# Local and global attention with a gated MLP on one Trainium2 core: batch 1 takes the chunk form of the later batches

## The chip, the cores and the metric

The kernel runs on one core of one Trainium2 chip. The core has five engines that run on their own and meet at semaphores: TensorE (PE: matmuls, with PEld for its weight loads), VectorE (DVE), ScalarE (ACT), GpSimd (POOL) and SyncE (SP). The metric is the device time of one execution in microseconds (us), as the median of the runs. The profile is of one execution of its own.

## The reference

Eight batches of eight heads; each head has 512 local and 32 global tokens of 64 dimensions. A global query attends to all 544 keys; a local query attends to the 32 global keys and to the local keys at a distance of at most 32. The result goes through a two-layer MLP (512 to 2048 to 512) with a quick-gelu between.

```python
k_all = concat([k_g, k_l]); v_all = concat([v_g, v_l])
out_g = softmax(scale * q_g @ k_all.T) @ v_all
mask = abs(pos[:, None] - pos[None, :]) <= 32
s_ll = where(mask, scale * q_l @ k_l.T, -1e9)
s_lg = scale * q_l @ k_g.T
out_l = softmax(concat([s_lg, s_ll])) @ concat([v_g, v_l])
x = concat([out_g, out_l]) as (B * S, H * D)
h = x @ w_in;  out = (h * sigmoid(1.702 * h)) @ w_out
```

## The kernel before, in words

**Tiling.** Four heads form a quad, so a batch has two (in the code `a` and `c`). Scores are computed with keys on the partitions and queries along the free dimension, in a first and a second round: `S(0)` and `S(1)` are the score matmuls, `X` the exponential on ACT, `M` the multiply with the 0/1 band mask, `U(0..2)` the matmuls that give the sum of the exponentials (unit 0, with a matrix of ones) and two halves of the output values, `Gm` the rows of the global queries, `R` the turned reciprocals of the sums, `XL` the normalised rows of x, `G` the global rows. `T`, `Tk` and `Tq` turn keys and queries by DVE transposes; `ext` puts the global queries (and keys) beside the local ones.

**Two forms of a quad.** Batches 0 and 1 use class `Quad`: four chunks of 128 local keys. The global keys are a part of their own: `gg` and `K` (both through `gk`, L367) compute their scores, `XK` (L417) the exponentials, `ekU` (L429) adds them to the sums, and `eg` (L398) spreads a small block for the global queries. Batches 2 to 7 use `Wide`: a chunk has 96 local and the 32 global keys, one chunk in five has 128 local keys, so the global keys need no step of their own. For it `Tk` copies a part of the turned keys (L525, called kcopy below), `Tq` copies a part of the queries (L535, qcopy), and `ext` writes the global keys between the local ones. The value tile (`load_v`, L97 and L99) holds the global value rows on partitions 96 to 127 of four of its five chunks, loaded four times from memory.

**The MLP.** `h_mm` and `h_step` (L624) are the first layer, 16 steps of four matmuls a batch; `h_act` is a tanh on ACT (L631) and a product on DVE (L632). `o_mm` (L649) is the second layer: four row blocks of 16 matmuls, here called output matmuls, and one copy on ACT (L663) for each block. `osteps` places quarters of a row block (four matmuls) between the parts of batch 1's attention.

**The order.** It is written out by hand: the schedule is manual, and each engine runs its instructions in the order of the program. Attention of batch b + 1 is woven into the output matmuls of batch b. All loads with a cast, so nearly all loads, go through POOL's queue (`load_rest`, then `load_v`, `load`, `load_g`): queries and keys of batch 1, the weights, the values of batch 1, queries and keys of batch 2, and so on. The program gives POOL's DMAs eight completion counters in turn, and each DMA waits on its counter's last user. Score banks: the pair of tiles `s0` and `s1` (four banks) from `spair()` is used by every score group in turn, and other stages borrow it; four more banks rotate under the name `p`.

**Batch 1 before.** ACT makes the two `near_mask` tables between the tanh's of batch 0 (L202). GpSimd makes the later batches' mask by six copies (L220) after the loads of batch 2's values. All four `M` of batch 1 are on DVE (L388). The transpose of batch 2's first queries stands in DVE's order between batch 1's second quad and its normalisation.

Of the kernel before, what the change touches and what calls it, by code (L numbers as in the profile page):

```python
# [20 lines left out]
def kernel(  # L21
# [68 lines left out]
    def load_v(b):  # L90
        if b < 4:
            nc.gpsimd.memset(v_view(b, 5)[:, :, :, :, D:], 1.0)
        vt = v_view(b, 5).rearrange("p u j c d -> p (u j) c d")
        vs, vg = (x[b].rearrange("h s d -> s h d") for x in (v_l, v_g))
        for c in range(5):
            n = 128 if c == 2 else 96
            nc.gpsimd.dma_start(out=vt[0:n, :, c, :D], in_=vs[FIRST[c] : FIRST[c] + n])  # L97
            if c != 2:
                nc.gpsimd.dma_start(out=vt[96:128, :, c, :D], in_=vg)  # L99

    rqg = consts.tile([128, NQ, D], BF16)
    rkg = consts.tile([128, NQ, D], BF16)

    rvg = consts.tile([128, 4, D + 2], BF16)

# [4 lines left out]

    def load_g(lo, hi, names="kqv"):
        for name, dst, src in (("k", rkg, kgf), ("q", rqg, qgf)):
            if name in names:
                nc.gpsimd.dma_start(out=dst[:, lo:hi, :], in_=src[:, lo:hi, :])
        if "v" in names:
            load_turned(nc.gpsimd, rvg[:, lo:hi, :D], vgf[:, lo:hi, :])

# [36 lines left out]
    for i in range(2):  # L154
        vtiles.append(consts.tile([128, 8 * 5 * (D + 2)], BF16, name="v%d" % i))
        nc.gpsimd.memset(v_view(i, 4)[:, :, :, :, D:], 1.0)
    nc.gpsimd.affine_select(
# [24 lines left out]
    WIN = ((0, 10), (6, 12), (14, 12), (22, 10))  # L182
    near_mask = consts.tile([128, 2, LW], BF16)
    mask = consts.tile([128, 2, MW], BF16)
# [14 lines left out]
    def make_near(c):
        nr = WIN[c][1]  # L200
        at = (0, 160, 0, 192)[c]
        nc.scalar.activation(near_mask[:, c // 2, at : at + 16 * nr].rearrange("p (t r) -> p t r", t=16),  # L202
                             near(bandt, c), AF.Copy)

# [41 lines left out]
    def load_rest():  # L246
        load_v2(0)
        n = d_ff // 4
        for part in range(4):
            for u in range(2):  # L250
                nc.gpsimd.dma_start(out=w_in_sb[:, part, 2 * u : 2 * u + 2],  # L251
                                    in_=w_in_r[u][:, :, part * n : part * n + n])
        for g4 in (1, 0, 2, 3):
            nc.gpsimd.dma_start(
                out=w_out_sb[:, 4 * g4 : 4 * g4 + 4, :].rearrange("p (g e) m -> p g (e m)", e=2),
                in_=w_out_r[:, 2 * g4 : 2 * g4 + 2, :])
            if g4 == 0:
# [9 lines left out]
        nc.gpsimd.dma_start(out=loaded[2][0], in_=kf[2])  # L267
        nc.gpsimd.dma_start(out=loaded[2][1][:, 1], in_=qf[2][:, 1])

# [13 lines left out]
    class Quad:  # L283
        def __init__(self, Q):
# [4 lines left out]
            self.x = xL[self.b]  # L289
            self.v = v_view(self.b, 4 if self.b < 2 else 5)[:, self.u]  # L290
            self.qt = qtiles[Q % 4]
# [78 lines left out]

        def X(self, rnd, between=None):
            e = self.E[rnd]
# [5 lines left out]
            for i in range(2):  # L378
                if i and between:
                    between()  # L380
                nc.scalar.activation(e[:, 2 * i : 2 * i + 2, :RW], self.ps[i][:, :, :RW], AF.Exp, scale=scale)  # L381
            if rnd == self.gr:
                nc.scalar.activation(e[:, 2, RW:], bank(self.ps, 2)[:, RW : RW + 32], AF.Exp, scale=scale)

        def M(self, rnd):
            at = 36 if rnd else 40
            e = self.E[rnd][:, :, at : at + LW]
            nc.vector.tensor_mul(e, e, near_mask[:, rnd : rnd + 1, :].to_broadcast([128, 4, LW]))  # L388

# [19 lines left out]

        def gg(self, rnd=0):  # L410
            self.gr = rnd
            self.gk(bank(self.ps if rnd else self.spt(0), 2)[:, RW : RW + 32], self.qg)


        def XK(self):
# [3 lines left out]
        def ekU(self, unit, ov=None):  # L419
# [4 lines left out]
            for j in range(4):  # L424
# [5 lines left out]
                                 start=first, stop=not first, skip_group_check=True)  # L430

        def ekUs(self, nxt=None, rnd=0, banks=(None, None, None)):
            if nxt:
                if rnd is not None:
                    nxt.gg(rnd)
                nxt.K(0)
            self.ekU(0, ov=banks[0])
            if nxt:
                nxt.K(1)
            self.ekU(1, ov=banks[1])  # L440
            self.ekU(2, ov=banks[2])

# [74 lines left out]
    class Wide(Quad):  # L517
        qc = None

        def Tk(self):  # L520
# [4 lines left out]
            nc.vector.tensor_copy(self.kT[:, 2:4, 0:96], self.kT[:, 0:2, 96:192])  # L525
            self.k = flat.bitcast(BF16).rearrange("p (m e) -> p m e", e=2)
# [304 lines left out]
    a.Tk()
    gTs[1] = moe.tile([128, FC, TB], BF16, name="gT")
    hps = [pbank("hp") for _ in range(2)]
    for fc, kcs in ((0, (0, 1)), (1, (0, 1)), (0, (2, 3)), (1, (2, 3))):
        h_mm(1, fc, hps[fc], kcs)
    pt = spair()
    hps += [bank(pt, j) for j in (2, 3, 0, 1)]
    for fc in range(2, 6):
        h_mm(1, fc, hps[fc], range(NKC))

    def on_act(out_, in_):
        nc.scalar.activation(out_, in_, AF.Copy)

    for fc in range(FC):
        if fc < 2:
            h_act(1, fc, hps[fc])
        elif fc in (2, 4):
            f = slice(fc, fc + 2)
            th = early[:, fc - 2 : fc]
            nc.scalar.activation(th, pt[1 - (fc - 2) // 2], AF.Tanh, scale=0.851)  # L850
            nc.vector.scalar_tensor_tensor(gTs[1][:, f, :], in0=th, scalar=1.0, in1=pt[1 - (fc - 2) // 2],
                                           op0=ALU.add, op1=ALU.mult)
        elif fc >= 6:
            h_step(1, fc)
        if fc == 1:
            transpose_g(4, 6, "q")
        if fc == 2:
            nq[1][1].G()
        if 3 <= fc <= 6:
            a.ext((fc - 3,), on_act)  # L860
        if 7 <= fc <= 9:
            c.ext((fc - 7,), on_act)
        if fc == 10:
            a.S(0)
            a.X(0, (0,))
        if fc == 11:
# [110 lines left out]
```

## Time and profile before

| what | value |
|---|---|
| time, median of 3 runs | 300.27 us (299.44 to 300.33) |
| the profiled execution's own time | 300.44 us |
| its span | 298.7 us |
| PE busy | 291.8 us, 98% of the span, 3407 matmuls |
| DVE busy | 217.1 us, 73% |
| ACT busy | 170.4 us, 57% |
| POOL busy | 80.4 us, 27% |
| DMA moved | 28.18 MB, mean 94 GB/s |

Times in the profile count from the start of the span. A line of a timeline holds start, duration, engine, source line, operation, output and inputs, the tile's shape, how many instructions are merged, and in brackets how long the engine stood idle before it and what ended that. Merged instructions overlap at their ends, so the step from one start to the next is the cost in sequence. The chain that ended last is followed back from the end of the program: each piece is what the next one waited for.

### The profile page before, as it was taken

Reading aid. Unit: us, or ns where it says so; the run is one execution under the profiler, and the core shown is the slowest. Engines: PE = TensorE matmul, PEld = TensorE weight load, DVE = VectorE, ACT = ScalarE, POOL = GpSimd, SP = SyncE. Lnnn points to the kernel's source line nnn. Section 1 sums busy time; section 2 is a strip of 40 time slices with the busy share of each in tenths; the row PEclk is TensorE's granted clock in tenths of the full one; section 3 lists DMA queues with packets and bytes.
Section 4 is the critical chain, followed back from the end, with each engine's and each line's share of the span. In section 5 each row is a group of like instructions: output and inputs, shape, how many; then the busy total and the mean of one; then the engine's idle time right before and its main releaser. Section 6 shows DMA issues by size and latency. Waiting matters only on the chain.

```text
span 298.7 us, 8149 instructions
## 1 busy us (share of the span) xinstructions
PE 291.8 (98%) x3407; PEld 150.1 (50%) x3407; DVE 217.1 (73%) x431; ACT 170.4 (57%) x280; POOL 80.4 (27%) x130
## 2 busy tenths in 40 slices
PE   7899999999999999999999999999999999999995
PEld 6444445445554455445454455445544455455653
DVE  7578857988978878797969878787879766683320
ACT  4838475397447736577357745676447651663421
POOL 8853655609754001800072003500000000000000
PEclk9999999999999999999999999999999999999999
DMA  7999999974999512980289114900230022101122
GB/s 204 162 196 210 188 168 217 151 137 28 149 204 155 106 37 63 131 144 20 54 81 187 36 38 82 116 0 16 59 72 0 2 54 56 35 1 28 45 69 72
DMA packets 59444, 28.18 MB, mean 94 GB/s; under 512 B 47504, under 2 KB 49808, under 8 KB 59408
## 3 DMA queue, kind: packets, MB, share of 16 engines
q0 software_dynamic: 51568, 17.57, 54.5%
q1 hardware_dynamic: 7360, 9.45, 12.1%
q10 hardware_dynamic: 480, 0.66, 0.7%
q8 instruction: 26, 0.43, 0.6%
q14 instruction: 10, 0.08, 0.1%
HBM read 36.31 MB, written 8.91 MB: 151 GB/s over the span
## 4 chain that ended last, share of the span: by engine, by line
PE 79%; DMA 12%; POOL 3%; DVE 3%; issue 1%; ACT 1%; ACTq 0%; DVEq 0%; POOLq 0%
PE op L649 33%; PE hp L624 33%; DMA rk<-in_k_l_dram 7%; PE ov L595 5%; PE s L569 4%; DMA rq<-in_q_l_dram 3%; DMA w_in_sb<-in_moe_w_in_dram 3%; PE s L624 1%; POOL v L244 1%; DVE xL L488 1%; PE op L661 1%; PE og L606 1%; DVE rs L483 0%; POOL w_in_sb L251 0%; ACT ob L663 0%
## 5 line engine op out<-in xcount | busy, mean ns | idle before, releaser
L649 PE MATMUL op<-w_out_sb,gT 128*128 128x512 bf16 x528 | 121.7, 380 | 0.0
L632 DVE SCALAR_TENSOR_TENSOR gT<-th,hp 128x512 bf16<-128x512 f32 (+1 forms) x136 | 87.0, 655 | 36.0 <-ACT th L631 35.5
L624 PE MATMUL hp<-xL,w_in_sb 128*128 128x512 bf16 x480 | 105.6, 379 | 0.2 <-DVE xL L488 0.2
L631 ACT ACTIVATE th<-hp 128x512 f32<-128x512 f32 (+1 forms) x136 | 77.5, 573 | 36.7 <-PE hp L624 34.0
L624 PEld LDWEIGHTS <-w_in_sb 128*128 128x128 bf16 x576 | 56.1, 98 | 64.7 <-issue 0.8
L649 PEld LDWEIGHTS <-gT 128*128 128x128 bf16 x528 | 49.3, 98 | 55.3 <-issue 0.9
L663 ACT ACTIVATE ob<-op 128x512 f32<-128x512 f32 (+2 forms) x35 | 20.4, 587 | 70.1 <-PE op L649 67.6
L97 POOL DMA_DIRECT2D v<-in_v_l_dram x30 | 24.0, 801 | 84.7 <-PE og L606 79.4
L580 ACT ACTIVATE e<-s 128x1016 bf16<-128x1016 f32 (+1 forms) x48 | 45.8, 1005 | 0.0
L585 DVE TENSOR_TENSOR e<-e,mask 128x1712 bf16<-128x1712 bf16 (+1 forms) x23 | 23.9, 1040 | 2.7 <-ACT e L580 2.1
L479 DVE STREAM_TRANSPOSE sT<-ov 128x512 f32<-128x512 f32 x15 | 10.7, 714 | 16.2 <-PE ov L595 14.4
L488 DVE TENSOR_TENSOR xL<-ov,rs 128x512 bf16<-128x512 f32 x29 | 18.7, 686 | 1.6 <-PE ov L455 0.4
L569 PEld LDWEIGHTS <-kT 32*128 32x128 bf16 x576 | 10.6, 93 | 10.4 <-issue 7.6
L381 ACT ACTIVATE e<-s 128x856 bf16<-128x856 f32 x12 | 10.1, 888 | 7.4 <-PE s L348 7.4
L99 POOL DMA_DIRECT2D v<-in_v_g_dram x24 | 13.9, 579 | 1.6 <-DMA rk<-in_k_l_dram 1.1
L569 PE MATMUL s<-q,kT 32*128 32x160 bf16 (+1 forms) x384 | 12.6, 246 | 0.0
L309 DVE STREAM_TRANSPOSE q<-rq 128x512 f32<-128x512 f32 (+1 forms) x17 | 11.4, 669 | 1.6 <-DMA rq<-in_q_l_dram 1.4
L523 DVE STREAM_TRANSPOSE kT<-rk 128x512 f32<-128x512 f32 x12 | 12.5, 1042 | 0.0
L483 DVE STREAM_TRANSPOSE rs<-rT 128x512 f32<-128x512 f32 x16 | 11.4, 711 | 0.6
L595 PE MATMUL ov<-e,v 128*32 128x128 bf16 (+3 forms) x576 | 11.0, 223 | 0.0
L624 PE MATMUL hp<-xG,w_in_sb 128*128 128x256 bf16 x64 | 9.6, 273 | 0.0
L595 PEld LDWEIGHTS <-v 128*32 128x32 bf16 x576 | 9.1, 97 | 0.0
(113 smaller groups left out, 202.8 us busy)
## 6 DMA issues: line engine op xcount, KB each, us to landing
out_dram<-ob SPq DMA_DIRECT2D x132, 64.0 KB, 2.5
rk<-in_k_l_dram POOLq DMA_DIRECT2D x6, 512.0 KB, 9.6
rq<-in_q_l_dram POOLq DMA_DIRECT2D x5, 512.0 KB, 7.4
v<-in_v_l_dram POOLq DMA_DIRECT2D x24, 96.0 KB, 4.5
w_in_sb<-in_moe_w_in_dram POOLq DMA_DIRECT2D x8, 256.0 KB, 8.2
w_out_sb<-in_moe_w_out_dram POOLq DMA_DIRECT2D x4, 512.0 KB, 10.3
v<-in_v_l_dram POOLq DMA_DIRECT2D x14, 128.0 KB, 6.4
rq<-in_q_l_dram POOLq DMA_DIRECT2D x5, 256.0 KB, 9.9
```

Of the source, the lines that this page charges most:

```text
L97: nc.gpsimd.dma_start(out=vt[0:n, :, c, :D], in_=vs[FIRST[c] : FIRST[c] + n])
L99: nc.gpsimd.dma_start(out=vt[96:128, :, c, :D], in_=vg)
L488: nc.vector.tensor_mul(self.x[:, 2 * self.u + h, :], self.st[1 + h], self.st["rs"])
L569: nc.tensor.matmul(bank(self.ps, j)[:, at : at + n], lhsT=self.k[p, KEYS[c] : KEYS[c] + 128, e], rhs=qs[p, :, :, e], start=(e == 0), stop= ...
L580: nc.scalar.activation(self.E[rnd][:, 2 * i : 2 * i + 2, :n], self.ps[i][:, :, :n], AF.Exp, scale=scale)
L585: eng.tensor_mul(e, e, mask[:, rnd : rnd + 1, :n].to_broadcast([128, 4, n]))
L595: nc.tensor.matmul(ov[32 * j : 32 * j + 32, :].rearrange("p (t r) -> p t r", t=16)[:, t0:t1, r0 : r0 + nr], lhsT=lv, rhs=self.E[rnd][:, j, ...
L624: nc.tensor.matmul(hp[:, : width(i)], lhsT=w_in_c[:, fc // 4, kc, fc % 4 // 2, :, fc % 2], rhs=(xL[i] if i < B else xG)[:, kc, :], start=( ...
L631: nc.scalar.activation(th[:, :n], hp[:, :n], AF.Tanh, scale=0.851)
L632: nc.vector.scalar_tensor_tensor(gTs[i][:, fc, :n], in0=th[:, :n], scalar=1.0, in1=hp[:, :n], op0=ALU.add, op1=ALU.mult)
L649: nc.tensor.matmul(op, lhsT=gTs[i][:, fc, tci * 128 : tci * 128 + 128], rhs=w_out_sb[:, fc, :], start=(first and fc == 4 * f4), stop=(fc = ...
L663: nc.scalar.activation(ob[:, lo:hi], op[:, lo:hi], AF.Copy, scale=0.5)
```

## The change

- Batch 1 becomes `Wide`: `nq = {1: (Wide(2), Wide(3)), ...}`. `gg`, `K`, `XK`, `eg`, `ekU` and `near_mask` are gone for it (`Quad` stays for batch 0).
- For its first quad, `ext`, kcopy and qcopy are done by ACT; for the second quad by DVE. The first rounds' masks of both quads are multiplied by GpSimd (`M(0, nc.gpsimd)`), the second rounds' by DVE.
- Its value tile has five chunks. The global value rows are loaded once (`load_vg1`) and copied by two ACT instructions into the other chunks (`copy_vg1`, between the exponentials of the first quad's two rounds). Its values come by five loads of 96 or 128 keys instead of four, one for each quad and half of the partitions.
- The six mask copies on GpSimd move to the load sequence, ahead of the last quarter of w_in.
- The loads of batch 2's keys and second queries move behind the first GpSimd multiply, those of batch 2's values and batch 3 behind the second.
- Batch 2's transposes and copies move behind the first products of batch 1's MLP, some of them from DVE to ACT; c's `Gm` now stands ahead of its `U`, the output quarters between the parts are placed anew, and the first eight h steps are held in four rotating and four score banks instead of two and four.

```diff
     def load_v(b):
-        if b < 4:
+        if b == 2:
...
-            if c != 2:
+            if c != 2 and b != 1:
                 nc.gpsimd.dma_start(out=vt[96:128, :, c, :D], in_=vg)
+    def load_vg1():
+        vt = v_view(1, 5).rearrange("p u j c d -> p (u j) c d")
+        nc.gpsimd.dma_start(out=vt[96:128, :, 0, :D], in_=v_g[1].rearrange("h s d -> s h d"))
+    def copy_vg1():
...
+        on_act(vt[96:128, :, 1:2, :D], src)
+        on_act(vt[96:128, :, 3:5, :D], src.to_broadcast([32, 8, 2, D]))
...
         for part in range(4):
+            if part == 3:
+                for m in MASKS:
+                    make_mask(m)
...
                 load(1, (0,))
                 load_g(2, 4)
+                load_vg1()
...
-        load_v2(1)
+        load_v(1)
         load(2, kq=False)
         nc.gpsimd.dma_start(out=loaded[2][1][:, 0], in_=qf[2][:, 0])
-        load_g(4, 8, "k")
-        load_g(4, 8, "q")
-        nc.gpsimd.dma_start(out=loaded[2][0], in_=kf[2])
-        nc.gpsimd.dma_start(out=loaded[2][1][:, 1], in_=qf[2][:, 1])
+        load_g(4, 8)
...
-        if fc in (5, 6, 8, 9):
-            make_near((5, 6, 8, 9).index(fc))
...
-    load_v(2)
-    for part in MASKS:
-        make_mask(part)
-    load(3)
...
-    nq = {1: (Quad(2), Quad(3)), 2: (Wide(4), Wide(5))}
+    nq = {1: (Wide(2), Wide(3)), 2: (Wide(4), Wide(5))}
     a, c = nq[1]
-    a.T()
     transpose_g(2, 4)
-    a.ext()
-    osteps(0, (0, 1), (0, 0), (1, 1), (1, 0), (2, 1))
+    a.Tk(False)
+    a.Tq(False)
+    a.ext((0, 1, 2), on_act)
+    a.kcopy(on_act)
+    a.ext((3,), on_act)
+    a.qcopy(on_act)
+    osteps(0, (0, 1), (0, 0), (1, 1), (1, 0), (2, 1), (2, 0))
     a.S(0)
-    a.gg()
-    a.K()
     a.X(0)
-    a.XK()
-    a.M(0)
-    a.eg()
-    c.T()
+    a.M(0, nc.gpsimd)
+    nc.gpsimd.dma_start(out=loaded[2][0], in_=kf[2])
+    nc.gpsimd.dma_start(out=loaded[2][1][:, 1], in_=qf[2][:, 1])
+    copy_vg1()
+    c.Tk()
+    c.Tq()
     c.ext()
-    osteps(0, (2, 0), (0, 2), (1, 2))
+    osteps(0, (0, 2), (1, 2), (2, 2))
     a.S(1)
     a.X(1)
     a.M(1)
-    osteps(0, (2, 2), (0, 3))
+    osteps(0, (0, 3), (1, 3))
     c.S(0)
     c.X(0)
-    c.M(0)
-    nq[2][0].Tq()
-    transpose_g(4, 6, "k")
-    osteps(0, (1, 3), (2, 3))
+    c.M(0, nc.gpsimd)
+    load_v(2)
+    load(3)
+    osteps(0, (2, 3), (3, 0))
     c.S(1)
-    a.ekUs(c, 1)
-    c.X(1, lambda: c.XK())
+    c.X(1)
     for unit in range(3):
         a.U(unit)
     a.R()
     c.M(1)
-    c.eg()
+    osteps(0, (3, 1), (3, 2), (3, 3))
     pt = spair()
-    a.Gm(bank(pt, 0)[:, 0 : D + 2])
-    osteps(0, (3, 0), (3, 1))
     a.XL(0)
     a.XL(1)
-    c.ekUs(banks=[bank(pt, unit + 1) for unit in range(3)])
-    for unit in range(3):
-        c.U(unit)
+    a.Gm(bank(pt, 1)[:, 0:128])
+    c.Gm(bank(pt, 1)[:, 128:256])
+    c.U(0, bank(pt, 0))
     c.R()
+    c.U(1, bank(pt, 2))
+    c.U(2, bank(pt, 3))
     c.XL(0)
     c.XL(1)
...
+    hps = [pbank("hp") for _ in range(4)]
+    for kcs in ((0, 1), (2,), (3,)):
+        for fc in range(4):
+            h_mm(1, fc, hps[fc], kcs)
     a.G()
-    c.Gm()
-    osteps(0, (3, 2), (3, 3))
+    c.G()
+    pt = spair()
+    for fc in range(4, 8):
+        h_mm(1, fc, bank(pt, (fc - 2) % 4), range(NKC))
...
         if fc == 1:
-            transpose_g(4, 6, "q")
+            transpose_g(4, 6)
+            a.Tk(False)
+        if fc in (2, 3):
+            a.ext((fc - 2,), on_act)
+        if fc == 3:
+            a.Tq(False)
+        if fc == 4:
+            a.kcopy(on_act)
+            a.ext((2,), on_act)
+        if fc == 6:
+            a.ext((3,), on_act)
+            a.qcopy(on_act)
...
         if i == 1:
-            c.Tk()
-        c.Tq()
-        if i > 1:
+            c.Tk(False)
+            c.Tq(False)
+        else:
+            c.Tq()
             c.ext((3,))
         a.S(1)
         a.X(1)
         if i == 1:
+            c.ext((0, 1, 2), on_act)
+            c.kcopy(on_act)
             c.ext((3,), on_act)
+            c.qcopy(on_act)
```

More of the change, by code (lines that the diff above doesn't have):

```diff
@@ L97, in load_v, with on_act @@
             nc.gpsimd.dma_start(out=vt[0:n, :, c, :D], in_=vs[FIRST[c] : FIRST[c] + n])
-            if c != 2:
+            if c != 2 and b != 1:
                 nc.gpsimd.dma_start(out=vt[96:128, :, c, :D], in_=vg)
+    def load_vg1():
+        vt = v_view(1, 5).rearrange("p u j c d -> p (u j) c d")
+        nc.gpsimd.dma_start(out=vt[96:128, :, 0, :D], in_=v_g[1].rearrange("h s d -> s h d"))
+    def copy_vg1():
+        vt = v_view(1, 5).rearrange("p u j c d -> p (u j) c d")
+        src = vt[96:128, :, 0:1, :D]
+        on_act(vt[96:128, :, 1:2, :D], src)
+        on_act(vt[96:128, :, 3:5, :D], src.to_broadcast([32, 8, 2, D]))
+    def on_act(out_, in_):
+        nc.scalar.activation(out_, in_, AF.Copy)
     rqg = consts.tile([128, NQ, D], BF16)
     rkg = consts.tile([128, NQ, D], BF16)
-    rvg = consts.tile([128, 4, D + 2], BF16)
+    rvg = consts.tile([128, 2, D + 2], BF16)
     def load_turned(eng, out_, in_):
@@ L109, in load_turned, with load_g @@
         eng.dma_start(out=out_[0:32], in_=in_[96:128])
-    def load_g(lo, hi, names="kqv"):
+    def load_g(lo, hi, names="kq"):
         for name, dst, src in (("k", rkg, kgf), ("q", rqg, qgf)):
@@ L114, in load_g @@
                 nc.gpsimd.dma_start(out=dst[:, lo:hi, :], in_=src[:, lo:hi, :])
-        if "v" in names:
-            load_turned(nc.gpsimd, rvg[:, lo:hi, :D], vgf[:, lo:hi, :])
     g32 = {}
@@ L155 @@
         vtiles.append(consts.tile([128, 8 * 5 * (D + 2)], BF16, name="v%d" % i))
-        nc.gpsimd.memset(v_view(i, 4)[:, :, :, :, D:], 1.0)
+        nc.gpsimd.memset(v_view(i, 4 + i)[:, :, :, :, D:], 1.0)
     nc.gpsimd.affine_select(
@@ L182 @@
     WIN = ((0, 10), (6, 12), (14, 12), (22, 10))
-    near_mask = consts.tile([128, 2, LW], BF16)
     mask = consts.tile([128, 2, MW], BF16)
@@ L197, in near @@
         return t[:, :, lo : lo + WIN[c][1]]
[L199 to L203, printed above, removed]
     MASKS = (
@@ L289, in __init__ @@
             self.x = xL[self.b]
-            self.v = v_view(self.b, 4 if self.b < 2 else 5)[:, self.u]
+            self.v = v_view(self.b, 5 if self.b else 4)[:, self.u]
             self.qt = qtiles[Q % 4]
@@ L369, in gk, with X @@
                                      start=(ee == 0), stop=(ee == 1), skip_group_check=True)
-        def X(self, rnd, between=None):
+        def X(self, rnd):
             e = self.E[rnd]
@@ L378, in X @@
             for i in range(2):
-                if i and between:
-                    between()
                 nc.scalar.activation(e[:, 2 * i : 2 * i + 2, :RW], self.ps[i][:, :, :RW], AF.Exp, scale=scale)
[L382 to L388, printed above, removed]
         def K(self, e=None):
@@ L408, in spt @@
             return self.pt
-        def gg(self, rnd=0):
-            self.gr = rnd
-            self.gk(bank(self.ps if rnd else self.spt(0), 2)[:, RW : RW + 32], self.qg)
         def XK(self):
@@ L430, in ekU @@
                                  start=first, stop=not first, skip_group_check=True)
[L432 to L441, printed above, removed]
         def U(self, unit):
@@ L518, with kcopy, qcopy, Tk @@
         qc = None
-        def Tk(self):
+        def kcopy(self, copy):
+            copy(self.kT[:, 2:4, 0:96], self.kT[:, 0:2, 96:192])
+        def qcopy(self, copy):
+            copy(self.qc[:, 4:20].bitcast(BF16), self.qt[:, 4:20, 10:22].bitcast(BF16))
+        def Tk(self, copy=nc.vector.tensor_copy):
             self.kT = att.tile([128, 4, 320], F32, name="kT", bufs=2)
@@ L524, in Tk @@
                                 loaded[self.b][0][:, self.u].bitcast(F32))
-            nc.vector.tensor_copy(self.kT[:, 2:4, 0:96], self.kT[:, 0:2, 96:192])
+            if copy:
+                self.kcopy(copy)
             self.k = flat.bitcast(BF16).rearrange("p (m e) -> p m e", e=2)
@@ L530, in near_q, with Tq @@
                 self.qc = att.tile([128, 20, 12], F32, name="qc", bufs=2)
-        def Tq(self):
+        def Tq(self, copy=nc.vector.tensor_copy):
             Quad.Tq(self)
             self.near_q()
-            nc.vector.tensor_copy(self.qc[:, 4:20].bitcast(BF16), self.qt[:, 4:20, 10:22].bitcast(BF16))
+            if copy:
+                self.qcopy(copy)
         def ext(self, parts=range(4), copy=None):
@@ L814 @@
     c.M(1)
-    c.eg()
+    osteps(0, (3, 1), (3, 2), (3, 3))
     pt = spair()
-    a.Gm(bank(pt, 0)[:, 0 : D + 2])
-    osteps(0, (3, 0), (3, 1))
     a.XL(0)
     a.XL(1)
-    c.ekUs(banks=[bank(pt, unit + 1) for unit in range(3)])
-    for unit in range(3):
-        c.U(unit)
+    a.Gm(bank(pt, 1)[:, 0:128])
+    c.Gm(bank(pt, 1)[:, 128:256])
+    c.U(0, bank(pt, 0))
     c.R()
+    c.U(1, bank(pt, 2))
+    c.U(2, bank(pt, 3))
     c.XL(0)
     c.XL(1)
+    gTs[1] = moe.tile([128, FC, TB], BF16, name="gT")
@@ L827 @@
+    hps = [pbank("hp") for _ in range(4)]
+    for kcs in ((0, 1), (2,), (3,)):
+        for fc in range(4):
+            h_mm(1, fc, hps[fc], kcs)
     a.G()
-    c.Gm()
-    osteps(0, (3, 2), (3, 3))
+    c.G()
+    pt = spair()
+    for fc in range(4, 8):
+        h_mm(1, fc, bank(pt, (fc - 2) % 4), range(NKC))
     a, c = nq[2]
[L831 to L842, printed above, removed]
     for fc in range(FC):
-        if fc < 2:
+        if fc < 4:
             h_act(1, fc, hps[fc])
-        elif fc in (2, 4):
+        elif fc in (4, 6):
             f = slice(fc, fc + 2)
-            th = early[:, fc - 2 : fc]
-            nc.scalar.activation(th, pt[1 - (fc - 2) // 2], AF.Tanh, scale=0.851)
-            nc.vector.scalar_tensor_tensor(gTs[1][:, f, :], in0=th, scalar=1.0, in1=pt[1 - (fc - 2) // 2],
+            th, ps = early[:, fc - 4 : fc - 2], pt[1 - (fc - 4) // 2]
+            nc.scalar.activation(th, ps, AF.Tanh, scale=0.851)
+            nc.vector.scalar_tensor_tensor(gTs[1][:, f, :], in0=th, scalar=1.0, in1=ps,
@@ L852 @@
                                            op0=ALU.add, op1=ALU.mult)
-        elif fc >= 6:
+        elif fc >= 8:
             h_step(1, fc)
         if fc == 1:
-            transpose_g(4, 6, "q")
[L857 to L862, printed above, removed]
+            transpose_g(4, 6)
[4 more added lines that the diff above has]
+            a.Tq(False)
@@ L870 @@
             load(4)
-            load_g(8, NQ, "kq")
+            load_g(8, NQ)
     def phase_o(i):
```

## The prediction

> **What bounds the kernel now.** I read first the page's busy times and the slices of the span, then the chain that ended last in order of time, then the timelines of PE, ACT, POOL and DVE between 32 and 72 us, where batch 1's attention runs.
>
> ```profile
> PE 291.8 (98%) x3407; PEld 150.1 (50%) x3407; DVE 217.1 (73%) x431; ACT 170.4 (57%) x280; POOL 80.4 (27%) x130
> ...
> DMA  7999999974999512980289114900230022101122
> ```
>
> PE is busy nearly all the time, so a gain must be PE work that goes or one of its few waits. The DMA engines are full until about 60 us (the first eight slices of 7.5 us). The chain shows where a landing, not PE, decided:
>
> ```profile
> 37.62 9.89 DMA rq<-in_q_l_dram
> ...
> 47.53 0.72 DVE q L309
> ...
> 54.25 1.30 DVE xL L488 x2
> ...
> 55.59 0.81 PE hp L624 x3
> ...
> 64.17 0.58 PE s L569 x23
> ...
> 69.17 0.56 PE s L569 x23
> ```
>
> Batch 2's query load lands at 47.5; its transpose stands in DVE's queue ahead of batch 1's normalisation, so batch 1's last xL comes late and the h matmuls of batch 1, begun at 54.03 (52.25 + 8 x 0.222), lose 0.64: their first eight last from 54.03 to 56.40 instead of 8 x 0.216 = 1.73. I measure the change at the last line: batch 2's second score group now starts at 69.17, and behind it everything is one steady run of PE work, the same in both kernels.
>
> **PE work.** The timeline gives the old form of batch 1 (the separate global-key work is L367 and L429):
>
> ```profile
> 36.92 0.66 PE L348 MATMUL s<-q,kT 32*128 32x200 bf16 x16
> 37.51 0.22 PE L367 MATMUL s<-qgT,kgT 32*32 32x32 bf16 x8
> 37.58 0.62 PE L367 MATMUL kb<-q,kgT 32*32 32x512 bf16 x8
> ...
> 50.85 0.68 PE L455 MATMUL s<-e,ones 128*32 128x160 bf16 x16
> ```
>
> From start to next start: four score groups 0.59 + 0.60 + 0.59 + 0.59, global scores 0.62 (36.92's group ends at 37.51, next work at 38.13), the mixed global stretch 46.27 to 47.07 = 0.80, ekU 50.10 to 50.85 = 0.75, U 0.93 and 1.12, Gm 0.27 and 0.28: 7.14. The new form is read from batch 2 in the chain: 0.56 + 0.58 + 1.20 + 0.16 = 2.50 a quad, 5.00 for both. So 2.14 of PE work goes; the 64 output matmuls stay (64 x 0.2224 = 14.23). If nothing waited, h would begin at 32.44 + 14.23 + 5.00 = 51.67 and the mark come 13.82 + 0.57 later, at 66.1: 3.1 sooner, of which 0.64 is the lost wait and 0.3 small gaps. The question is what of it other engines leave.
>
> **ACT.** The four near_mask copies go (about 0.4 each between tanh's, off PE's path: worth nothing, PE was full there). Batch 1's exponentials grow, and copies come:
>
> ```profile
> 41.52 1.66 ACT L381 ACTIVATE e<-s 128x856 bf16<-128x856 f32 x2 [1.67 <-PE s L348]
> ...
> 69.77 1.89 ACT L580 ACTIVATE e<-s 128x992 bf16<-128x992 f32 x2
> ```
>
> The wide first round takes 1.93 (73.90). At the start qgT is out at 34.7, kT at 35.9, q at 36.6 (DVE's transposes from 34.53); the three small copies, kcopy (192 elements, between the rows of 0.30 and 0.60; I take 0.35), 0.42 and qcopy 0.5 end by 37.2, before a.S(0) at 37.78 (24 instead of 20 output matmuls first). So they cost nothing; without those four extra matmuls, 0.3. a.X(0) runs 38.4 to 40.35. The two global-value copies have no row on 32 partitions; by their 512 and 1024 elements they take 0.6 and 1.0 (rows of 128 partitions; a quarter of that if partitions counted). I take the full price: a.X(1) then runs 41.8 to 43.7, and c.S(0), due at 43.36, has its last two banks at 43.7. Then two output copies (0.5 each) and c.X(0), 44.55 to 46.5; c.S(1), due at 46.06, ends at 47.1; c.X(1) ends at 49.15. ACT thus costs PE 0.9 here. The copies moved to ACT in batches 1 and 2's second quads (about 1.8 after a.X(1)) end just as c.S(0) of batch 2 wants them, 0 to 0.3; I take 0.
>
> **POOL and the loads.** POOL is one queue, and each of its DMAs waits for the landing of the one eight issues back:
>
> ```profile
> 39.36 0.75 POOL L114 DMA_DIRECT2D rqg<-in_q_g_dram  x1 [0.38 <-DMA rk<-in_k_l_dram]
> 42.37 0.70 POOL L267 DMA_DIRECT2D rk<-in_k_l_dram  x1 [2.25 <-DMA w_out_sb<-in_moe_w_out_dram]
> ...
> 67.40 3.32 POOL L585 TENSOR_TENSOR e<-e,mask 128x1760 bf16<-128x1760 bf16 x1 [8.41 <-issue]
> ```
>
> The last w_out load, issued at 33.67, lands 8.4 later, at 42.07; now the eighth issue behind it is rk, in the new kernel (five value loads instead of four) it is rqg. So rqg is issued at 42.1 to 42.8, and behind it stands the first GpSimd mask: 42.8 to 46.1 (3.32), though its exponentials are there at 40.35. Then the two loads of batch 2 (0.70 + 0.57), then the second mask, 47.45 to 50.75. Its first reader, c.Gm, is due at 51.24: the multiplies on GpSimd are just hidden by themselves. The six mask copies (2.33, from 55.30) now stand ahead of the third w_in pair. POOL spent over 5 us waiting for landings between 14.6 and 24.7, and at 16.4 five w_in loads are still in flight, the last landing at 22.7: I take 0, and 2.3 if that cover is gone. The value loads and vg are as many bytes as before and land by 46.6, and the first value matmuls start at 47.6. rk of batch 2 is issued 3.7 later but queues behind loads until 48.4; its transpose comes at 58. The nine value loads of batch 2 and load(3) now follow the second multiply, 50.8 to about 58.5, for readers from 71 on: 0.
>
> **DVE.** Batch 1's second quad is transposed when its rk lands (39.1) and, with six copies, ready by 42.2, ahead of c.S(0): 0; a load later by more than 1.2 would show there.
>
> **Where GpSimd and DVE meet.** Four DVE copies that met a POOL DMA issue (ending at 36.86) lasted 0.36 to 0.61 each and ended together at 36.87 to 36.89; alone the same four took 0.43 in all:
>
> ```profile
> 35.21 1.65 POOL L244 DMA_DIRECT2D v<-in_v_l_dram  x2
> ...
> 36.26 0.63 DVE L319 COPY q<-qgT 128x40 f32<-128x40 f32 x4
> ...
> 41.73 0.43 DVE L319 COPY q<-qgT 128x40 f32<-128x40 f32 x4
> ```
>
> A POOL multiply beside a DVE multiply has no row: each DVE mask may cost its 1.05, or wait for the POOL multiply's end. I take the wait, since the nearest row shows one. [...] Then a.M(1), ready at 43.7, runs 46.1 to 47.15, and a.U starts at 47.2, which costs 0.1. c.M(1), ready at 49.4 behind a.R, runs 50.75 to 51.8, and c.Gm waits from 51.24 to 51.85. DVE then does a.XL (1.3), c.R (1.75), c.XL (0.65 each): third kc at 55.5, where PE wants it at 54.95; last xL at 56.1.
>
> **The end of the stage.** Behind it DVE owes, without a pause, two G (1.3), four products (2.4), transposes (0.35 + 1.05 + 0.65) and two double products (1.1 each): 7.95, until 64.05, since the score banks of batch 2 are the ones that the second double product reads. PE could start that score group at 63.4. Then 0.57 and 20 matmuls (4.32): the mark at 69.0 against 69.17. The sum: -3.1 (PE and old waits) + 0.9 (ACT) + 0.1 + 0.6 (c.Gm) + 0.6 (xL) + 0.7 (banks) = -0.2. The profiled execution took 300.44 (span 298.7), 0.17 above the median of 300.27; so **300.44 - 0.2 - 0.17 = 300.1**.
>
> **Rivals.**
> - *The multiplies run side by side.* c.M(1) then ends at 50.45, c.Gm and xL do not wait, last xL at 54.9, banks at 62.85, mark at 67.8: -1.4, **298.9**. For it: the products (L632) at 67.8 to 69.8 kept their 0.68 beside POOL's multiply, but one of their inputs is in PSUM. Against: the copies above.
> - *All is hidden,* with short ACT copies and banks in time: -3.1, **297.2**. Against it: DVE's 7.95 hardly shrinks.
> - *POOL's queue comes late:* slower. If the 2.33 of mask copies is not absorbed, w_out lands at 44.4, both POOL multiplies and all behind them move by 2.3: **302.4**; half of it gives 301.2. It decides from 1.1 of lateness on. For it: c.Gm already waits on that chain, so each us counts in full. Against: POOL's waits at 17 to 32 us, and full DMA engines.
> - *No net effect by other small waits,* near 300.3.
>
> **Chances.** About 0.3% (0.9 us) is what a measurement of this kernel can tell from no change. Forecast 0.47 (of it 0.08 faster, 0.33 same, 0.06 slower), side by side 0.25 (0.21 faster, 0.04 same), all hidden 0.05 (faster), late queue 0.15 (0.13 slower, 0.02 same), small waits 0.08 (0.02, 0.04, 0.02). Faster 0.36, same 0.43, slower 0.21. The range goes from between the second and third case, 298.4, to 301.6 on the side of the late queue.
>
> **What would show it.** In the new profile: two POOL multiplies at about 43 and 47.5, the first behind rqg, waiting for w_out; the DVE mask beside each lasting 2 us or more, or starting late (right), or 1.05 beside it (first rival); exponentials of ACT back to back from 38 to 49; PE waiting at c.S(0), c.S(1), c.Gm and at batch 2's first score group; U with 72 matmuls in 1.20. Wrong would be: w_out landing after 43, value loads after 47.6, or h of batch 1 beginning later than 54.

## The result and the profile after

The changed kernel takes 301.38 us (median of 22 runs, 300.15 to 304.46); the kernel before, run beside it, 299.67 (22 runs, 299.28 to 302.28). The ratio is 1.0063, interval 1.004 to 1.0086: **slower by 0.6%**, where 300.1 was forecast against 300.27. The profiled execution took 303.67 (span 302.0) and is one of five, of 22, in which the mean granted clock was 0.989 to 0.994 instead of 0.998 to 1.0; those five took 303.2 to 304.5, the other 17 took 300.15 to 301.9. So the profile shows the loss in its strongest form, and a second profile of the same kernel (below) is read beside it. Of one later kernel (the loads of batch 2 ahead of the first multiply) four runs of twelve were over 1.5% above its fastest, 305.8 to 306.5, and its ratio is that of the other eight.

The page of after, busy times and slices:

```profile
PE 288.5 (96%) x3390; PEld 150.2 (50%) x3431; DVE 215.0 (71%) x421; ACT 173.1 (57%) x284; POOL 87.1 (29%) x131
...
PEclk9999999799999999999999999999999999999999
DMA  7999999950999711990269512900220012101113
```

PE is busy for 3.3 us less than before (291.8), and yet the span is 3.3 longer: PE stands idle. The timeline of PE in after shows where (in brackets: idle time before, and what ended it):

```profile
43.77 0.53 PE L557 MATMUL s<-q,kT 32*128 32x160 bf16 x14 [0.25 <-ACT e L568]
...
46.57 0.28 PE L557 MATMUL s<-qc,kT 32*128 32x108 bf16 x6 [0.18 <-ACT e L568]
...
51.36 0.55 PE L583 MATMUL s<-e,ones 128*32 128x128 bf16 x24
51.73 0.75 PE L583 MATMUL s<-e,v 128*32 128x128 bf16 x38
54.71 0.35 PE L583 MATMUL s<-e,v 128*32 128x72 bf16 x10 [2.23 <-issue]
54.99 5.32 PE L612 MATMUL hp<-xL,w_in_sb 128*128 128x512 bf16 x15
...
66.85 0.53 PE L557 MATMUL s<-q,kT 32*128 32x160 bf16 x16 [0.50 <-DVE gT L830]
```

In the middle of the 72 value matmuls of the second quad PE stops for 2.23 us, after 62 of them, and goes on with the last ten. The first 14 matmuls of `U(2)` had run, and `U(1)` had read all the exponentials that the last ten read again. "issue" says that the profile shows nothing that PE waited for. Batch 1's h begins at 54.99 instead of the 53.3 forecast. The chain that ended last has the same pause in its midst:

```profile
51.54 0.94 PE s L583 x62
52.48 2.23 issue
54.71 0.35 PE s L583 x10
55.06 0.76 PE hp L612 x3
```

There is a second pause later, behind batch 2's first values (timeline of PE):

```profile
78.64 0.39 PE L637 MATMUL op<-w_out_sb,gT 128*128 128x512 bf16 x1 [0.67 <-DVE rT L461]
```

PE's last matmul ended at 77.97 and this one began at 78.64: 0.67. The profile puts the wait down to a reciprocal on DVE, but that had ended at 78.15, 0.49 before. In a kernel below (the split kernel) the same matmul starts at 74.21, right behind the values, while that reciprocal lasts until 74.45; so it does not wait for it.

**The measure of the prediction**, the start of batch 2's second score group, is 69.10 in the timeline of PE of before and 71.84 in after. (The chain puts it 0.07 later in both; below, "the mark" is the timeline's.) The row of before, then that of after:

```profile
69.10 0.28 PE L569 MATMUL s<-qc,kT 32*128 32x108 bf16 x8
...
71.84 0.28 PE L557 MATMUL s<-qc,kT 32*128 32x108 bf16 x8
```

**Where the loads and multiplies came.** POOL's timeline of after:

```profile
40.55 0.74 POOL L127 DMA_DIRECT2D rqg<-in_q_g_dram  x1 [1.71 <-DMA w_out_sb<-in_moe_w_out_dram]
41.31 3.33 POOL L573 TENSOR_TENSOR e<-e,mask 128x1760 bf16<-128x1760 bf16 x1
...
46.61 3.32 POOL L573 TENSOR_TENSOR e<-e,mask 128x1760 bf16<-128x1760 bf16 x1 [0.72 <-ACT e L568]
```

rqg did wait for w_out, but that landed at 40.27, 1.8 sooner than assumed, so both multiplies ended before anything needed them. DVE's two masks beside them (DVE's timeline of after):

```profile
43.82 1.74 DVE L573 TENSOR_TENSOR e<-e,mask 128x1712 bf16<-128x1712 bf16 x1 [3.30 <-ACT e L568]
...
49.40 1.43 DVE L573 TENSOR_TENSOR e<-e,mask 128x1712 bf16<-128x1712 bf16 x1
```

Alone this multiply takes 1.04 (a row of it stands below). Here each ended about 0.9 behind the end of GpSimd's: 45.56 against 44.64, and 50.83 against 49.93. They were held, as forecast.

**PE had run out of instructions.** The trace lists a DMA queue of kind "instruction", and the page of after counts it:

```profile
q8 instruction: 27, 0.44, 0.6%
```

Twenty-seven packets of 16 KB. By the page's 3390 matmuls and 3431 weight loads, a packet holds about 253 of these, some 127 pairs of a weight load and a matmul (an estimate from these three counts, which takes all 27 packets for PE's). Counted along PE's program, the two pauses stand at its 734th and 988th weight load, 254 = 2 x 127 apart. From the starts and durations of the single packets, and with the blocks laid so that one ends at each pause (in before, which has none, by the same count of loads, so its two entries are good to some tenths of a us):

| kernel, profile | PE enters the block of loads 607 to 733 | next packet runs | PE has used up the block | PE goes on |
|---|---|---|---|---|
| before | 48.00 | 51.36 to 52.34 | 57.53 | at once |
| after | 48.01 | 52.31 to 53.27 | 52.48 | 54.71 |
| after, second profile | 48.61 | 52.44 to 53.37 | 53.08 | 54.69 |

In before, too, the packet comes 3.4 us after the block is entered, but there the block holds many long matmuls (0.216 each) and lasts 9.5 us. In after it holds 116 small matmuls (8 to 17 ns each: `Gm` 0.33 for 40, `U` 1.20 for 72) beside 11 long ones, and is used up in 4.5 us. PE goes on 1.4 us after the packet's end, at both pauses (53.27 to 54.71; 77.24 to 78.64). My theory from here: **the denser form eats its instructions faster than they come.** The rivals: the wait hides some data (loads, the ACT copies, a mask), or it is the late clock that costs.

### The profile page after: what moved, and what is told of

Same layout as the page of the kernel before. It is cut to its first block, busy times and chain, and to the rows that moved or that the text cites. A ratio compares the mean times of both kernels' runs of the same rounds, so it can differ in the third digit from the quotient of the medians.

```text
span 302.0 us, 8148 instructions
## 1 busy us (share of the span) xinstructions
PE 288.5 (96%) x3390; PEld 150.2 (50%) x3431; DVE 215.0 (71%) x421; ACT 173.1 (57%) x284; POOL 87.1 (29%) x131
## 4 chain that ended last, share of the span: by engine, by line
PE 85%; ACT 4%; DVE 3%; issue 2%; ACTq 0%
PE hp L612 36%; PE op L637 35%; PE ov L583 5%; PE s L557 5%; ACT e L568 2%; PE s L612 1%; DVE gT L620 1%; ACT ob L651 1%; DVE gT L830 1%; PE op L649 1%; PE og L594 1%; ACT v L112 1%; PE s L583 0%; DVE e L573 0%; DVE kT L509 0%
## 5 line engine op out<-in xcount | busy, mean ns | idle before, releaser
L637 PE MATMUL op<-w_out_sb,gT 128*128 128x512 bf16 x498 | 119.1, 379 | 2.4 <-DVE rT L461 0.7
L568 ACT ACTIVATE e<-s 128x1016 bf16<-128x1016 f32 (+1 forms) x56 | 53.5, 1006 | 2.0 <-PE s L557 1.9
L97 POOL DMA_DIRECT2D v<-in_v_l_dram x35 | 28.3, 815 | 82.3 <-PE og L594 81.5
L573 DVE TENSOR_TENSOR e<-e,mask 128x1712 bf16<-128x1712 bf16 (+1 forms) x25 | 27.1, 1082 | 6.0 <-ACT e L568 5.4
L557 PEld LDWEIGHTS <-kT 32*128 32x128 bf16 x672 | 12.8, 93 | 13.2 <-issue 9.7
L557 PE MATMUL s<-q,kT 32*128 32x160 bf16 (+1 forms) x448 | 15.0, 246 | 0.8 <-DVE gT L830 0.5
L509 DVE STREAM_TRANSPOSE kT<-rk 128x512 f32<-128x512 f32 x14 | 14.6, 1039 | 1.6 <-DMA rk<-in_k_l_dram 1.6
L573 POOL TENSOR_TENSOR e<-e,mask 128x1760 bf16<-128x1760 bf16 x3 | 10.0, 3322 | 12.9 <-issue 12.2
L583 PEld LDWEIGHTS <-v 128*32 128x32 bf16 x672 | 10.5, 97 | 2.4 <-issue 2.4
```

The lines of the kernel that those rows point to most:

```text
L557: nc.tensor.matmul(bank(self.ps, j)[:, at : at + n], lhsT=self.k[p, KEYS[c] : KEYS[c] + 128, e], rhs=qs[p, :, :, e], start=(e == 0), stop= ...
L568: nc.scalar.activation(self.E[rnd][:, 2 * i : 2 * i + 2, :n], self.ps[i][:, :, :n], AF.Exp, scale=scale)
L573: eng.tensor_mul(e, e, mask[:, rnd : rnd + 1, :n].to_broadcast([128, 4, n]))
L583: nc.tensor.matmul(ov[32 * j : 32 * j + 32, :].rearrange("p (t r) -> p t r", t=16)[:, t0:t1, r0 : r0 + nr], lhsT=lv, rhs=self.E[rnd][:, j, ...
L637: nc.tensor.matmul(op, lhsT=gTs[i][:, fc, tci * 128 : tci * 128 + 128], rhs=w_out_sb[:, fc, :], start=(first and fc == 4 * f4), stop=(fc = ...
```

## The experiments

A ratio compares a kernel with the runs of before that were timed beside it. The medians of these are 300.03 (23 runs), 299.67 (35) and 299.66 (30).

**The changed kernel again.** No edit.

> The changed kernel once more. Theory A (PE runs out of instructions in the dense stretch of small matmuls at 48 to 52.5 us, because the next 16 KB block of its program comes over the loaded DMA engines; the pause then halves PE's granted clock for some us): the pause sits at the same matmul pair (the 734th) with 1 to 3 us, whether or not the clock drops; time 300 to 304, about 0.6% above before. Theory B (a data wait that the profile does not name: a landing or a bank): the pause has the same place too; this run alone does not tell them apart, it gives the spread.

301.67, ratio 1.0053 (1.0033 to 1.0073). Its profile (span 300.4, clock 0.999), timeline of PE:

```profile
52.32 0.76 PE L583 MATMUL s<-e,v 128*32 128x128 bf16 x38
54.69 0.35 PE L583 MATMUL s<-e,v 128*32 128x72 bf16 x10 [1.61 <-issue]
54.97 3.63 PE L612 MATMUL hp<-xL,w_in_sb 128*128 128x512 bf16 x15
```

The pause is at the same matmul, 1.61 long, and again at the 988th load, 0.85. The clock stayed full: the 15 h matmuls took 3.63 here and 5.32 in the first profile. That 1.7 is the whole difference of the two marks (70.13 and 71.84). So the halved clock comes on top, and the pauses come without it.

**Other places of the block ends.** A hundred matmuls of batch 0's MLP, all ahead of the pauses, are each made two of half the columns. That adds 100 pairs ahead of batch 1, and so moves every block's end within its matmuls; the work is the same.

```diff
...
+            n = width(i)
+            w_ = n // 2 if i == 0 and fc >= 4 else n
+            for lo in range(0, n, w_):
...
+                                 rhs=(xL[i] if i < B else xG)[:, kc, lo : lo + w_],
...
+            w_ = 256 if i == 0 and (tci < 3 or st == 12) else 512
+            for lo in range(0, 512, w_):
...
```

> 100 matmuls of batch 0's MLP, all before 46 us, are split in two of half the columns: the same arithmetic and about the same PE time, but every later instruction stands 100 pairs further back in the program, so that the block of about 127 pairs that now begins at 48.0 and runs dry at 52.5 begins with the pair that ran at 45.0 and ends with the one at 51.1. Theory A: the fetch has 6 us instead of 4.5, the pause of 2.2 shrinks below 0.6, PE's clock stays at 1.0, h of batch 1 begins near 52.7 instead of 55.0; time about 298.5 to 299.5. Theory B: no data moved, the pause stays at 52.5 with 2.2 us; time 301.4.

This first form sets the start flag for both halves of a bank, and its output is off by a relative 0.115: part of those sums is left out. 299.24, ratio 0.9978 (0.9966 to 0.999); no pause, mark at 68.31. The form with one start flag for a bank:

> The split of the run before with the accumulation flags set so that each half adds up rightly; the instructions, their number and their order are the same. Theory A: as in that run, no pause behind the second quad's U and none at the next block's end (76 us), clock 1.0, time 299.0 to 299.6, about 0.8% below the changed kernel. If that run's gain came from its arithmetic, this one is at 301.4.

299.34, ratio 0.9994 (0.9981 to 1.0008). Timeline of PE:

```profile
51.54 0.55 PE L583 MATMUL s<-e,ones 128*32 128x128 bf16 x24
51.90 0.91 PE L583 MATMUL s<-e,v 128*32 128x128 bf16 x48
52.74 3.44 PE L615 MATMUL hp<-xL,w_in_sb 128*128 128x512 bf16 x13
```

Both pauses are gone, the mark is at 68.15, and the time is 2.0 us below the changed kernel's, which had lost 1.7. Below, this is "the split kernel". Nothing that the value matmuls read was touched, which speaks against a hidden wait for data. The packet behind the new block's entry at 44.52 came at 44.96, the next (51.22) at 51.59.

**The same split in the kernel before.**

> The same split in the kernel before, as a control for the split itself: 100 more matmul pairs before 46 us, the same arithmetic. Theory A: in the kernel before no block runs dry, so the split brings nothing unless it puts a boundary into a dense stretch: within 0.4 of before. If splitting matmuls is a gain of its own (weights loaded twice, finer waits), about 0.8 faster than before.

299.96, ratio 1.0004 (0.9994 to 1.0014): the split by itself brings nothing. Its mark is at 68.33, though, 0.77 sooner than in the profile of before: PE had no 0.64 at 55.

**Long matmuls between the small ones.** Of the changed kernel, the first two parts of four h steps are put between `c.U(0)` and `c.U(1)`, and `Gm` behind `U`.

```diff
+    c.U(0, bank(pt, 0))
+    c.R()
...
+    for fc in range(4):
+        h_mm(1, fc, hps[fc], (0, 1))
+    c.U(1, bank(pt, 2))
+    c.U(2, bank(pt, 3))
     a.Gm(bank(pt, 1)[:, 0:128])
     c.Gm(bank(pt, 1)[:, 128:256])
-    c.U(0, bank(pt, 0))
-    c.R()
-    c.U(1, bank(pt, 2))
-    c.U(2, bank(pt, 3))
...
-    for kcs in ((0, 1), (2,), (3,)):
+    for kcs in ((2,), (3,)):
```

> Batch 1's first eight h matmuls now stand between the second quad's U(0) and U(1), and both Gm behind U(2): the block that ran dry holds 1.7 us more of long matmuls. Theory A: the pause shrinks from 2.2 to about 0.5 and sits at about the 734th pair again, now in Gm or behind it; clock mostly 1.0; time 298.5 to 299.5. Theory B (a wait of U for a landing or a bank): the pause stays in U(2), 1 to 2 us, time above 300.5.

300.92, ratio 1.0041 (1.0026 to 1.0057), where theory A had 298.5 to 299.5. The first pause is gone, as the theory says, with a wait of 0.45 for the last xL in its place, and the mark comes at 68.82. But the second pause grew to 1.55 (74.94 to 76.49): PE reaches the later block's end sooner, its packet came at 73.78 to 74.95, and the gain is given back there.

**The loads of batch 2 ahead of the first GpSimd multiply.**

```diff
+        nc.gpsimd.dma_start(out=loaded[2][0], in_=kf[2])
+        nc.gpsimd.dma_start(out=loaded[2][1][:, 1], in_=qf[2][:, 1])
         load_g(4, 8)
...
     a.M(0, nc.gpsimd)
-    nc.gpsimd.dma_start(out=loaded[2][0], in_=kf[2])
-    nc.gpsimd.dma_start(out=loaded[2][1][:, 1], in_=qf[2][:, 1])
```

> Batch 2's keys and second queries (1.5 MB) are issued ahead of the global queries and keys again, and so land before 50 instead of at 51 to 54; PE's program is the same to the instruction. Theory A with the cause of the late fetch in those loads: the 16 KB fetch, which is due at 48 when PE enters its last block and starts only at 52.3 behind them, starts at 49 to 51, and the pause of 1.6 to 2.2 at the 734th pair shrinks below 0.8; the later pause at the 988th pair (0.7 to 1.5) stays; time about 300. If the fetch is late for another reason (it always starts when PE has used a fixed part of its block), it stays at 52.3 and the pause with it.

The time is not clear: 299.38 to 302.63, ratio 1.0027 (1.0005 to 1.005), in the eight runs named above. The profile, of an execution of 299.63, is clear. Timeline of PE:

```profile
51.94 0.55 PE L585 MATMUL s<-e,ones 128*32 128x128 bf16 x24
52.31 0.91 PE L585 MATMUL s<-e,v 128*32 128x128 bf16 x48
53.15 1.90 PE L614 MATMUL hp<-xL,w_in_sb 128*128 128x512 bf16 x7
```

The same matmuls in the same blocks: entered at 48.59, and now the packet came at 49.36, 0.8 later instead of 4.3. No pause, mark at 68.56; nor is there one at the 988th load, where the expectation had kept it. So with the loads moved ahead the packet came 3.5 us sooner after the block's entry. In after and its second profile it came (52.31, 52.44) as the last 2 KB packets of batch 2's loads ran out (52.52, 52.55); here those ended at 48.51. But with the masks on DVE (next) they ended at 49.88 and the packet came only at 52.21, amid packets of values. That instruction packets queue behind loads is the author's estimate from these ends, and not shown; behind which, and why this kernel's times spread so far, stays open.

**The masks back on DVE.** Once in the changed kernel, once in the split one.

```diff
-    a.M(0, nc.gpsimd)
+    a.M(0)
...
-    c.M(0, nc.gpsimd)
+    c.M(0)
```

> All four masks of batch 1 on VectorE, none on GpSimd: the holds of the two VectorE multiplies beside GpSimd's (1.74 and 1.43 instead of 1.03) go, and GpSimd issues its loads 1 to 3 us sooner. Theory A: PE's order and density are unchanged, so a pause of 1 to 3 us remains at the 734th pair, longer if the earlier loads crowd the fetch; time within 0.5% of the changed kernel. Theory C (the rule of my forecast, that the multiplies hold each other, is what cost the gain): the stretch from the second quad's scores to the first h matmul gets at least 0.6 shorter, time 300.0 or below.

> The split kernel with all four masks of batch 1 on VectorE: what GpSimd's two multiplies cost or bring when no pause for instructions hides it. Theory C (my forecast's mechanism: the holds of 0.7 and 0.4 lie on the path): 0.3 to 0.7 faster than the split kernel with GpSimd. Rival (VectorE's queue gets the two multiplies' 2.1 and the holds were hidden): 0.2 to 0.8 slower.

301.74, ratio 1.0059 (1.0036 to 1.0082), with both pauses (1.72 and 1.47); split, 299.42, ratio 0.9995 (0.9983 to 1.0007), with none. Neither of the changes expected of the split kernel came: the masks on GpSimd cost nothing that the times tell and bring nothing, and with all masks on DVE the changed kernel's pauses stay, so the held multiplies are not the loss. On DVE the first mask stands ahead of the second quad's transposes, and `c.S(0)` waits 0.66 for their last copy in the split kernel; in the other it waits 0.89, until that copy and an output copy on ACT have both ended (44.10 and 44.14).

**A pause of PE without a change of its instructions.** Idle transposes on DVE ahead of the second quad's normalisation, in the kernel before; three, five and eight of them.

```diff
+    late = consts.tile([128, 512], F32)
+    nc.vector.memset(late, 0.0)
...
+    for _ in range(3):
+        nc.vector.transpose(late, late)
     c.XL(0)
```

> The kernel before with three idle transposes (0.71 each) on VectorE ahead of the second quad's xL of batch 1: PE waits there for about 2.3 us instead of 0.2 to 0.6, for data and not for instructions. If a PE pause of 2 us or more by itself halves the granted clock for some us (as in the profile of the changed kernel, 0.50 from 55.8 to 59.4 behind a pause of 2.2), the granted clock of the stretch behind shows 0.5 to 0.7 in the profile or in some runs, and the time is 2 to 4 above before. If the clock fell for another reason, it stays at 1.0 and the time is 1.8 to 2.2 above before.

> The kernel before with five idle transposes of 128x512 (1.05 us each) ahead of batch 1's second normalisation instead of three; the matmuls and their instruction blocks are those of before. The step with three left PE 1.05 us without work and the clock stayed at 1.0. If the length of PE's pause alone halves the clock (the changed kernel's 2.23 us did, its 1.61 us did not): PE idle 2.5 to 3.2 us near 55 and slices of 0.5 within some us behind it, the mark at 72 to 73. If the clock fell for another reason: the same pause, clock 1.0, mark at 71 to 71.5.

> The same with eight idle transposes: PE idle 5 to 6 us near 55. If the length of the pause halves the clock: 0.5 for some us behind it, the mark 1 to 2 us later than the pause alone gives (73.5 to 74.5). If not: clock 1.0 and the mark later only by the pause.

With three: 301.3, ratio 1.006 (1.0038 to 1.0081), PE idle for 1.05 and 0.22, clock 1.0, mark at 69.98. With five: 303.63, in one run, mark at 71.22. Timeline of PE:

```profile
57.12 0.38 PE L626 MATMUL hp<-xL,w_in_sb 128*128 128x512 bf16 x1 [2.54 <-DVE xL L490]
57.71 0.81 PE L626 MATMUL hp<-xL,w_in_sb 128*128 128x512 bf16 x3 [0.22 <-DVE xL L490]
58.36 3.62 PE L626 MATMUL s<-xL,w_in_sb 128*128 128x512 bf16 x16
```

The clock stayed at 1.0 (16 matmuls in 3.62), behind a pause longer than after's 2.23. With eight: 305.94, in one run, pause 4.79, and a halved clock; the mark is at 74.66, 1.4 later than the longer pause alone gives (71.22 + 4.79 - 2.54 - 0.22). Two windows of its trace (window; its length and the busy times of PE, PEld, DVE, ACT, POOL; granted clock; DMA share and GB/s):

```profile
58.50:58.75 0.25, 0.00 (x0) 0.00 (x0) 0.25 (x1) 0.00 (x0) 0.00 (x0) 1.00 0.99 188
...
62.00:62.25 0.25, 0.25 (x2) 0.10 (x1) 0.25 (x1) 0.13 (x1) 0.00 (x0) 0.50 1.34 254
```

The clock stood at 0.50 for 3.4 us here (58.89 to 62.31) and in after (55.97 to 59.38). So the clock was halved behind the pauses of 2.23 and 4.79, but their length alone does not tell: behind 2.54 it was not.

The traces show what sorts them. In each of the 16, the clock's changes are whole multiples of 3.413 us apart: in after it rises to 1.0 at 4.77, falls at 55.97, 15 such windows later, and rises again one window later. Laid out from the first rise, the windows sort without exception: the clock fell behind all 18 in which PE was busy for 39% or less of a window at full clock (16 of them at the programs' ends), and behind none with 46% or more. After's pause of 2.23 lay in one window (52.56 to 55.97, PE busy for 35%). The pause of 2.54 fell across two (52.21 to 55.62 with 69%, 55.62 to 59.03 with 50%), and the 1.61 of after's second profile left 64% (50.88 to 54.30). (The transposes took 0.72 each and not the 1.05 of the expectation.)

**The remaining waits of the split kernel.** First, batch 2's first scores and exponentials one h step later; second, the value copies on DVE behind `c.ext()`; third, both.

```diff
-        if fc == 10:
+        if fc == 11:
             a.S(0)
             a.X(0, (0,))
-        if fc == 11:
+        if fc == 12:
             a.X(0, (1,))
```

```diff
-        on_act(vt[96:128, :, 1:2, :D], src)
-        on_act(vt[96:128, :, 3:5, :D], src.to_broadcast([32, 8, 2, D]))
+        nc.vector.tensor_copy(vt[96:128, :, 1:2, :D], src)
+        nc.vector.tensor_copy(vt[96:128, :, 3:5, :D], src.to_broadcast([32, 8, 2, D]))
```

> The split kernel with batch 2's first score group one h step later, so that VectorE's double product has left the score banks. Forecast's term 'banks' (0.5 in the split kernel's profile): that wait goes and the mark (start of batch 2's second group) comes 0.4 to 0.5 sooner; time 298.8 to 299.0. Rival: the exponentials come later in turn and a.U or the next group waits instead; no change.

> The split kernel with the two copies of global value rows on VectorE (idle from 40.5 to 43.8) instead of ScalarE. Forecast's term 'ACT 0.9': a.X(1) starts 0 to 0.2 sooner than 41.8 only as far as its scores are there, so the waits at c.S(0) (0.20) and c.S(1) (0.16) mostly go, the mark comes 0.2 to 0.4 sooner; time 299.0 to 299.2. Rival: the copies meet GpSimd's multiply, hold VectorE until 44.6 and delay a.M(1): no gain.

> Both of these on the split kernel: if both terms stand, the mark 0.6 to 0.9 sooner than in the split kernel and 298.5 to 298.8, below before by 0.3%. If the two waits share one cause, no more than the better of the two.

| | time | ratio to before | waits left |
|---|---|---|---|
| scores later | 298.96 | 0.9983 (0.9967 to 1.0) | banks gone |
| copies on DVE | 299.09 | 0.9973 (0.9956 to 0.999) | `c.S(0)` gone, `c.S(1)` 0.16 |
| both | **298.45** | **0.996 (0.9944 to 0.9976)** | `c.S(1)` 0.16 |

Against the split kernel's 299.34 the one brings 0.4, the other 0.25, both 0.9: a version that beats before by 0.4%. The ratio's interval of each single step overlaps that of the split kernel, so for the single steps the marks speak: 68.15 in the split kernel, 67.92 with the copies on DVE, 67.40 with both. A wait for the last xL of 0.24 (below) is left in all three. The profile of "scores later" (an execution of 300.22) shows another place where DVE was held beside GpSimd. DVE's timeline:

```profile
41.55 3.90 DVE L540 COPY qc<-qgT 128x72 bf16<-128x72 bf16 x1
...
45.50 1.04 DVE L573 TENSOR_TENSOR e<-e,mask 128x1712 bf16<-128x1712 bf16 x1
```

and POOL's:

```profile
42.06 3.34 POOL L573 TENSOR_TENSOR e<-e,mask 128x1760 bf16<-128x1760 bf16 x1
```

The second quad's keys landed late in this execution, so its copies met GpSimd's multiply: a copy of 72 elements lasted 3.90 (to 45.45; the multiply to 45.40), and `c.S(0)` waited 2.24 for it and the next copy (so the mark of this execution is at 69.11). The prediction named that margin: "a load later by more than 1.2 would show there".

## Why the prediction was wrong, point by point

- **The step that failed** is the reading that PE, when not waiting for another engine, works: "The question is what of it other engines leave", and, for all that comes after the mark, "behind it everything is one steady run of PE work, the same in both kernels". The sum counted matmuls and their durations, not how fast they use up instructions; a wait of PE for its own instructions has no term in it, and the pauses are that wait: PE went on 1.3 to 1.6 us after a packet's end, and with the block ends moved both pauses were gone. Ahead of the mark the first pause costs 1.6 (in the first profile 2.23, and 1.7 more by the halved clock); behind it the second costs 0.67 to 1.55. The latter can be read off: the span less the mark is 229.6 in before and 229.4 in the split kernel, which have no pause; 230.2 in after (second pause 0.67), 230.3 in its second profile (0.85), 230.9 with the masks on DVE (1.47), 231.0 with the long matmuls between (1.55).
- **The sign that was named** came: "h of batch 1 beginning later than 54". It began at 54.99, for a reason that was not among the rivals; the slower one there, a late POOL queue, did not occur (w_out landed at 40.27). (The mask copies stand ahead of the fourth w_in pair, `part == 3`, and not of the third.)
- *PE work:* right. `U`'s 72 matmuls took 1.20 in the chain (47.20 to 48.40), the score groups 0.57 where nothing waited, and `Gm` with the second `U` 1.53 in the split kernel (51.21 to 52.74) for 0.32 + 1.20.
- *ACT, +0.9:* right. The two copies took 1.57 together (1.6 taken), the exponentials 1.89 to 1.96. The steps over `c.S(0)` and `c.S(1)` were 1.06 and 0.96 (43.28 to 44.34, 46.17 to 47.13) instead of 0.57, 0.88 more. Taking the copies off ACT gave back 0.23 by the marks.
- *The holds of DVE:* right in the rows (1.74 and 1.43), and without cost; their price in the sum, *c.Gm +0.6,* was wrong. POOL's chain came earlier, so the second multiply ended at 49.93, not 50.75, and `c.Gm` did not wait. *Late xL, +0.6:* 0.24 of it came. In the split kernel the first h matmul on the last xL starts at 54.73, right behind that xL in the chain, and 0.46 behind the matmul before it instead of 0.216; PE's bracket for idle time shows only 0.08 there.
- *Banks, +0.7:* 0.50 in the row, and 0.52 by the marks without and with the step that removes it (67.92 and 67.40).
- *The base.* The profile of before had a loss that its usual runs do not have. Its span is 298.7; the 24 of the last 30 runs of before with a mean clock of 0.997 or more have spans of 297.6 to 298.4, 14 of them 297.8 or less; and the nearly same kernel with the split had no wait at 55. A gain worked out from a wait of 0.64 in one execution was in large part no gain.
- *The sum as a whole.* In its own measure, from the profile of before, it was too small: it had the mark 0.2 sooner, and in the split kernel, which has no pause, it comes 0.95 sooner (69.10 to 68.15), since 0.6 of c.Gm, 0.36 of xL and 0.2 of the banks did not come (1.16 together, less two waits of 0.16 marked "issue", at 48.74 and 63.95, that the profile of before does not have). Against the usual runs of before the change without pauses takes 0.3 us less by the medians and 0.2 by the ratio, which is not told from nothing. That this agrees with the 0.2 forecast is luck: waits that did not come went against a gain that was not there.

## What to carry to other kernels

When a change puts more, smaller matmuls in a stretch, count the instructions too: here a block of 127 pairs that lasted 9.5 us was used up in 4.5, and the next was not there. A pause in the midst of one tile's matmuls, with "issue" as its only reason and the same number of instructions between two such places, was the mark of it here; 100 more pairs ahead of it took it away (both pauses, in the split kernel), which was also the test. And a wait seen in a single profile is worth its size only if the usual runs have it: compare the span of the profiled execution with theirs.

## What the runs showed of the hardware

- In after, 27 packets of 16 KB came through DMA queue q8, of kind "instruction"; that they are PE's is an estimate from the number of PE's instructions. The packet behind the entry of a block came 0.8 us later in one profile and 4.3 in another for the same block, when batch 2's loads were issued sooner or later; PE went on 1.3 to 1.6 us after its end (seven pauses in four profiles).
- The granted clock halved for 3.4 us behind pauses of 2.23 and 4.79 us of PE, and not behind 2.54 or 1.61. In the 16 traces its changes lie on a grid of 3.413 us, and it fell behind each window of that grid in which PE was busy for 39% or less, and behind none with 46% or more; so in these traces the place of a pause on the grid counted beside its length. The drop is not special to the change: six of the 30 runs of before beside the last three kernels had a mean clock of 0.994 (300.6 to 301.0, against some 299.5), as one such stretch in 300 us gives.
- A DVE copy of 72 elements that started 0.5 us ahead of a GpSimd multiply lasted until that ended: 3.90 us, against 0.17 for this copy in after (at 40.23). (When the copy started, at 41.55, GpSimd was still issuing a DMA, from 41.30 to 42.04; which of the two held it first is not told.)
